# Seven stream buffers instead of five, re-used V space, four row groups for all output matmuls, and zero stores moved out of the first attention of a forward-and-backward decode kernel

## The chip, the cores and the metric

The kernel runs on one core of a Trainium2 chip. The metric is device time in microseconds (us), the median over separate executions. Before the change it was 562.25 us (555.37 to 563.79, three runs). A profiled execution records every instruction and transfer; its span (first to last instruction) is about 2 us shorter than the time of the same run.

## The reference

One token goes through two attention layers (A) and two MLP layers (B), with shared weights, and then backwards. The outputs are the final row and the gradients of the input, both caches and all weights.

```python
W = 4096                         # window: the last 4096 of 32768 cache rows
def A(x, k_cache, v_cache, wq, wo):        # 32 query heads, 4 kv heads, Dh = 128
    q = heads(x @ wq)                      # wq: 1024 x 4096
    p = softmax(q @ k[last W].T * Dh**-0.5)
    return (p @ v[last W]) @ wo            # wo: 4096 x 1024
def B(x, w1, b1, w2):                      # w1: 1024 x 3584, w2: 3584 x 1024
    h = x @ w1 + b1
    return (h * tanh(softplus(h))) @ w2
x = x + A(layernorm(x)); x = x + B(layernorm(x))      # called A1 and B2 below
x = x + A(layernorm(x)); x = x + B(layernorm(x))      # called A3 and B4
out, vjp = jax.vjp(f, A_x, k_cache, v_cache, wq, wo, w1, b1, w2)
return (out, *vjp(grad_out))               # gradients of all eight, bf16
```

Because a layer occurs twice, every weight gradient is a sum of two outer products. The cache gradients are zero outside the window: 58.7 MB of zeros (112 stores of 512 KB) must be written and depend on nothing.

## The kernel before

wq and the windows of K and V stay in SBUF, and so do NR of the sixteen 512 KB chunks of wo. All of w1, all of w2 and the other wo chunks are streamed through NB rotating buffers, anew in each pass. The loads and the zero stores are issued in program order on one queue (SP); the results leave through POOL's queue.

```python
NB = 5          # stream buffers
NR = 8          # wo chunks that stay in SBUF
strm  = tc.tile_pool(name="strm", bufs=NB)
vpool = tc.alloc_tile_pool(name="vpool", bufs=1)          # V, 32 KB per partition

def zeros(n):                          # n zero stores, from a tile that is never written again
    for _ in range(min(n, len(zero_jobs))):
        nc.sync.dma_start(zero_jobs.pop(0), zt[:])

# attention, forward, last step: y = o @ wo
order = list(range(NR, NO)) + list(range(NR))             # streamed chunks first
for i, c in enumerate(order):
    w = wo_kept[c] if c < NR else wo_load(c)
    if i == NB - 1:
        zeros(Z["A1" if first else "A3"])
    fwd_rows2(yacc, w, c, o_bf, i == 0, i == NO - 1)

# MLP, backward through w1: transpose each chunk on the matrix engine, copy it back, use it
def T(i):
    w = w1_load(i)                     # 448 KB into a stream buffer
    zeros(1 if i % 8 == 7 else 0)
    xpose2([alt_blocks(w[:, 0:1024], 4), alt_blocks(w[:, 1024:1792], 3)])   # 14 transposes
def M(i, _): ...                       # 14 matmuls of one column
pipe(list(range(2 * TD)), T, M)

Z = dict(A1=6, B2=1, A3=18, B4=1, bw2=19)
# [cut] ... after the last attention backward:
zeros(1000)                            # the final flush: all that are left

# output stage. R holds the two row vectors of a gradient at partitions 32*q, q = 0..3
def dw_tall(R, nblk, out_v):           # the gradients of w2 and wo
    for c in range(nblk // 2):
        st = stage_tile([P, 2, D], "st_t")
        pss = [psum2([P, 1024], FP32, "ops") for _ in range(2)]
        for i in range(2):
            for tt in range(2):
                b = 2 * c + tt
                outer(R, b % 4, (b // 4) * P, i * 512, pss[tt][:, i * 512:(i + 1) * 512])
        for tt in range(2):
            ev_out(st[:, tt, :], pss[tt][:])      # PSUM to SBUF on VectorE or ScalarE, in turn
        nc.gpsimd.dma_start(out_v[c], st[:])

def dkv(x3, y3, x1, y1, out_t):        # the gradients of K and V: two row groups (k = 0, 1) at a time
    for gp in range(2):
        for c0 in range(0, NC, 2):
            # [cut] two stage tiles; per four column blocks two 1024-wide PSUM tiles, 32-row matmuls at
            # row group c0 + k, two evictions of 128 x 1024; then two stores of 512 KB

stg = [0]
def stage_tile(shape, name):           # ten store tiles: five of their own, five stream buffers
    stg[0] += 1
    if stg[0] % 10 < 5:
        return shaped(pools["stage"].tile(...), shape)
    return shaped(strm.tile(...), shape)
```

Of the kernel before, what the change touches and what calls it, by code (L numbers as in the profile page):

```python
# [14 lines left out]
P = 128  # L15
HQ = 32
DH = 128
G = 4
NB = 5
NR = 8  # L20


@with_exitstack
def kernel(
# [116 lines left out]
    def shaped(t, shape):  # L141
        n = 1
        for k in shape[1:]:
            n *= k
        ap = t[0:shape[0], 0:n]
        if len(shape) == 3:
            return ap.rearrange("p (a b) -> p a b", a=shape[1])
        if len(shape) == 4:
            return ap.rearrange("p (a b c) -> p a b c", a=shape[1], b=shape[2])
        return ap  # L150

# [142 lines left out]
    def row_layout(col32, name):  # L294
        x = work.tile([P, G, DH], BF16, name=name, tag="rx", bufs=2)
        ps = psum1([P, P], BF16, "rps")
        nc.tensor.transpose(ps[:, 0:P], col32[:], ident_bf[:])
        for g in range(G):
            nc.vector.tensor_scalar(out=x[:, g, :], in0=ps[:, 0:P], scalar1=gmask[:, g:g + 1], scalar2=None, op0=ALU.mult)  # L299
        return x  # L300
# [227 lines left out]
    def attn_bwd(g_col, g_bf, lname, sv, first, nxt):  # L528
# [27 lines left out]
        big = psum2([P, WC], FP32, "big")  # L556
        rows_mm(big, pad, V_t)
        scr = work.tile([P, WC], BF16, name="scr", tag="e32", padded_shape=[P, 2 * WC])
        sdp = work.tile([P, 1], FP32, name="sdp")
# [5 lines left out]
        nc.vector.tensor_copy(sd[:], lps[:])  # L565
        ds = keep.tile([P, WC], BF16, name=f"ds_{lname}")
        nc.vector.scalar_tensor_tensor(out=ds[:], in0=big[:], scalar=sd[:, 0:1], in1=sv["p"][:], op0=ALU.subtract, op1=ALU.mult)
# [24 lines left out]
    def new_rows(name):  # L592
        return pools["rows"].tile([P, 2, 1024], BF16, name=name, tag="rows")

    def rows_put(R, side, kind, how):

        src, spread_t = pairs[kind], pools["spread"]
        spread = spread_t[:].rearrange("p j (q x) -> p j q x", q=4)
        for l in range(2):
            c = src[:, l, :]  # L600
            if how == "rep":
                nc.vector.tensor_copy(spread[:, :, :, l], c[:, :, None].to_broadcast([P, 8, 4]))
            elif how == "blocks":
                n = src.shape[2] // 4
                nc.vector.tensor_copy(spread[:, 0:n, :, l], c.rearrange("p (j q) -> p j q", q=4))
            elif how == "heads":
                for a in range(2):
                    nc.vector.tensor_copy(spread[:, 4 * a:4 * a + 4, :, l], c[:, 16 * a:16 * a + 16].rearrange("p (q b) -> p b q", q=4))
            else:
                for a in range(2):  # L610
                    v = c[:, 14 * a:14 * a + 14]
                    nc.vector.tensor_copy(spread[:, 4 * a:4 * a + 4, 0:3, l], v[:, 0:12].rearrange("p (q b) -> p b q", q=3))
                    nc.vector.tensor_copy(spread[:, 4 * a:4 * a + 2, 3, l], v[:, 12:14])
# [7 lines left out]
    def stage_tile(shape, name):  # L621
        stg[0] += 1
        if stg[0] % 10 < 5:
            return shaped(pools["stage"].tile([P, 2048], BF16, name=name, tag="so"), shape)
        return shaped(strm.tile([P, 2048], BF16, name=name, tag="st"), shape)

    def ev_out(out_ap, in_ap):
        evac(out_ap, in_ap, 1.22, 1.05)

    def outer(R, q, lo, ro, ps):  # L630
        mm(ps, R[32 * q:32 * q + 2, 0, lo:lo + P], R[32 * q:32 * q + 2, 1, ro:ro + ps.shape[1]], True, True, tile_position=(32 * q, 0))

    def dw_tall(R, nblk, out_v):

        for c in range(nblk // 2):
            st = stage_tile([P, 2, D], "st_t")
            pss = [psum2([P, 1024], FP32, "ops") for _ in range(2)]
            for i in range(2):
                for tt in range(2):
                    b = 2 * c + tt  # L640
                    outer(R, b % 4, (b // 4) * P, i * 512, pss[tt][:, i * 512:(i + 1) * 512])
            for tt in range(2):
# [3 lines left out]
    def dkv(x3, y3, x1, y1, out_t):  # L646
        ov = out_t[0, :, Sk - W:, :].rearrange("g (p t) d -> p g t d", p=P)
        for gp in range(2):
            for c0 in range(0, NC, 2):
                sts = [stage_tile([P, 2, TJ, DH], "st_kv") for _ in range(2)]  # L650
                for j4 in range(TJ // 4):
                    pss = [psum2([P, 4, 2, DH], FP32, "ops") for _ in range(2)]
                    for jj in range(4):
                        j = 4 * j4 + jj
                        for lay, (x, y) in enumerate(((x3, y3), (x1, y1))):
                            for k in range(2):
                                c = c0 + k
                                mm(pss[k][:, jj, :, :].rearrange("p g d -> p (g d)"), x[32 * c:32 * c + 32, j * P:(j + 1) * P],
                                   y[32 * c:32 * c + 32, 2 * gp:2 * gp + 2, :].rearrange("p g d -> p (g d)"), lay == 0 and jj % 2 == 0, lay == 1,
                                   tile_position=(32 * c, 0))  # L660
                    for k in range(2):
                        ev_out(sts[k][:, :, 4 * j4:4 * j4 + 4, :].rearrange("p g t d -> p t g d"), pss[k][:])
                for k in range(2):
                    nc.gpsimd.dma_start(ov[:, 2 * gp:2 * gp + 2, (c0 + k) * TJ:(c0 + k + 1) * TJ, :], sts[k][:])  # L664

    rows = {}

    def after_v():
        vpool.release()
        pools["rows"] = ctx.enter_context(tc.tile_pool(name="rows", bufs=2))  # L670
        pools["stage"] = ctx.enter_context(tc.tile_pool(name="stage", bufs=5))
        pools["spread"] = pools["rows"].tile([P, 8, P], BF16, name="spread", tag="spread", bufs=1)
        nc.gpsimd.memset(pools["spread"][:], 0.0)
        rows["w2"] = new_rows("R2")
        rows_put(rows["w2"], 0, "a", "blocks")
        rows_put(rows["w2"], 1, "gB", "rep")

    Z = dict(A1=6, B2=1, A3=18, B4=1, bw2=19)

# [66 lines left out]
    pt.release()  # L746
    pools["p2"] = ctx.enter_context(tc.tile_pool(name="p2", bufs=4, space=bass.MemoryType.PSUM))


    dw_tall(rows["w2"], TF, out_8.rearrange("(c p t) d -> c p t d", p=P, t=2))  # L750
    rows["w1"] = new_rows("R1")
    rows_put(rows["w1"], 0, "nB", "rep")
    rows_put(rows["w1"], 1, "dh", "pieces")
    for t in range(TD):
# [11 lines left out]
    rows["wo"] = new_rows("Ro")  # L766
    rows_put(rows["wo"], 0, "o", "blocks")
    rows_put(rows["wo"], 1, "gA", "rep")
    dw_tall(rows["wo"], HQ, out_5.rearrange("(c p t) d -> c p t d", p=P, t=2))
    do3 = row_layout(sA3["dorep"][:].rearrange("p c x -> p (c x)"), "do3x")  # L770
    do1 = row_layout(sA1["dorep"][:].rearrange("p c x -> p (c x)"), "do1x")
    dkv(sA3["p"], do3, sA1["p"], do1, out_3)
    q3 = row_layout(sA3["qrep"][:].rearrange("p c x -> p (c x)"), "q3x")
    q1 = row_layout(sA1["qrep"][:].rearrange("p c x -> p (c x)"), "q1x")
    dkv(sA3["ds"], q3, sA1["ds"], q1, out_2)
    rows["wq"] = new_rows("Rq")
    rows_put(rows["wq"], 0, "nA", "rep")
    rows_put(rows["wq"], 1, "dq", "heads")
    for t in range(TD):
# [39 lines left out]
```

## Time and profile before

| | before |
|---|---|
| time, median of 3 (us) | 562.25 |
| span of the profile (us) | 560.3 |
| bytes moved (MB), mean rate (GB/s) | 188.76, 337 |
| matrix engine, VectorE, ScalarE busy | 69%, 41%, 34% |
| mean granted clock of the matrix engine | 0.671 |

From the page of the kernel before: the span, busy time by engine (us, share, count), and the span in 40 equal slices: granted clock and busy share of the 16 DMA engines in tenths (9 is 90% or more), and GB/s.

```profile
span 560.3 us, 15939 instructions
PE 384.5 (69%) x7058; PEld 305.6 (55%) x7058; DVE 228.9 (41%) x411; ACT 192.4 (34%) x211; POOL 51.0 (9%) x95
...
PEclk9996555555569996677976599767755555555555
DMA  8999989999799979789599888896998978797986
GB/s 306 416 418 408 414 301 381 400 400 416 265 384 388 409 243 321 259 282 322 205 363 405 351 277 295 273 349 216 418 414 361 383 308 323 305 341 255 301 349 251
```

No engine is busy throughout. Transfers run at up to 418 GB/s, but not all the time: 188.76 MB at 415 GB/s would take 455 us, so by this estimate about 105 us of transfer time are lost, forward (slices 1 to 14) in a few gaps, backward (15 to 30) almost everywhere.

**Forward.** What the matrix engine waited for between 58 and 81 us, the last step of the first attention (columns: total, times, longest):

```profile
PE acc L188 <- DMA wo_c<-in_A_wo_dram: 16.2, 8, 8.1
```

The load queue's timeline (start, duration, what, count) shows why one wait lasts 8.1 us: six zero stores are issued between the fifth and the sixth streamed wo chunk.

```profile
47.67 5.45 SPq L255 DMA_DIRECT2D wo_c<-in_A_wo_dram  x5
54.13 6.68 SPq L129 DMA_DIRECT2D out_dram<-zt  x6
61.77 2.86 SPq L255 DMA_DIRECT2D wo_c<-in_A_wo_dram  x3
```

**Backward.** Part of the first backward w1 pass in the timeline; "tps" are the 14 transposes of a chunk, "acc" its 14 matmuls, and the brackets tell idle time before them:

```profile
244.43 0.96 PE L168 MATMUL tps<-ident_bf,w_c 128*128 128x128 bf16 x14 [1.12 <-DMA w_c<-in_B_w_dram]
245.23 0.49 PE L188 MATMUL acc<-dh_pair,w_c 128*128 128x1 bf16 x14
247.53 1.68 PE L168 MATMUL tps<-ident_bf,w_c 128*128 128x128 bf16 x14 [1.81 <-DMA w_c<-in_B_w_dram]
249.00 0.56 PE L188 MATMUL acc<-dh_pair,w_c 128*128 128x1 bf16 x14
249.42 1.65 PE L168 MATMUL tps<-ident_bf,w_c 128*128 128x128 bf16 x14
250.87 0.56 PE L188 MATMUL acc<-dh_pair,w_c 128*128 128x1 bf16 x14
```

The engine waits for loads, and after the 1.81 us wait the same 14 transposes take 1.68 instead of 0.96 us: the clock has dropped to half. At half clock the chunks' matmuls start 1.87 us apart (249.00 to 250.87); elsewhere in this pass, without waits and at full clock, 1.14 us. The windows view of both w1 passes (length, then busy time of PE, PEld, DVE, ACT, POOL with counts, granted clock, DMA share, GB/s):

```profile
235.40:263.00 27.60, 20.94 (x422) 20.34 (x420) 10.90 (x17) 10.65 (x13) 0.00 (x0) 0.81 0.84 276
346.00:373.00 27.00, 19.93 (x400) 19.24 (x397) 10.68 (x18) 10.01 (x12) 0.00 (x0) 0.81 0.88 293
```

Neither the matrix engine (20.9 of 27.6 us) nor DMA (276 GB/s) is full.

**Output.** The two groups of evictions of the w2 and wo gradients, from the groups view (count, busy us, mean ns, idle before), and one window of that stage:

```profile
L136 DVE CAST st_t<-ops 128x1024 bf16<-128x1024 f32 x28 | 33.0, 1220 | 6.9 <-issue 3.3
L139 ACT CAST st_t<-ops 128x1024 bf16<-128x1024 f32 x32 | 31.3, 1014 | 23.4 <-PE ops L188 21.6
```
```profile
430.00:440.00 10.00, 8.47 (x32) 1.56 (x32) 9.09 (x8) 9.34 (x10) 4.06 (x8) 0.50 0.81 315
```

VectorE and ScalarE are over 90% busy there, with one eviction each per chunk. In dkv the matrix engine works in two row groups; the timeline shows a pair of 256-column matmuls each 0.21 us:

```profile
496.57 0.44 PE L188 MATMUL ops<-do3x,p_A_2001 32*128 32x256 bf16 x2
496.78 0.45 PE L188 MATMUL ops<-do1x,p_A_681 32*128 32x256 bf16 x2
497.00 0.44 PE L188 MATMUL ops<-do3x,p_A_2001 32*128 32x256 bf16 x2
```

### The profile page before, as it was taken

Reading aid. Unit: us, or ns where it says so; the run is one execution under the profiler, and the core shown is the slowest. Engines: PE = TensorE matmul, PEld = TensorE weight load, DVE = VectorE, ACT = ScalarE, POOL = GpSimd, SP = SyncE. Lnnn points to the kernel's source line nnn. Section 1 sums busy time; section 2 is a strip of 40 time slices with the busy share of each in tenths; the row PEclk is TensorE's granted clock in tenths of the full one; section 3 lists DMA queues with packets and bytes.
Section 4 is the critical chain, followed back from the end, with each engine's and each line's share of the span. In section 5 each row is a group of like instructions: output and inputs, shape, how many; then the busy total and the mean of one; then the engine's idle time right before and its main releaser. Section 6 shows DMA issues by size and latency. Waiting matters only on the chain. (4 is left out here: it accounts for less than half of the span.)

```text
span 560.3 us, 15939 instructions
## 1 busy us (share of the span) xinstructions
PE 384.5 (69%) x7058; PEld 305.6 (55%) x7058; DVE 228.9 (41%) x411; ACT 192.4 (34%) x211; POOL 51.0 (9%) x95
## 2 busy tenths in 40 slices
PE   3384254364589979877966688768675756888790
PEld 3373153362589979867954677768362112146510
DVE  2052000102037753334632155324304866977691
ACT  1041000001027733333530144323102786855591
POOL 2000000000000000000000000000001423433341
PEclk9996555555569996677976599767755555555555
DMA  8999989999799979789599888896998978797986
GB/s 306 416 418 408 414 301 381 400 400 416 265 384 388 409 243 321 259 282 322 205 363 405 351 277 295 273 349 216 418 414 361 383 308 323 305 341 255 301 349 251
DMA packets 51041, 188.76 MB, mean 337 GB/s; under 512 B 5888, under 2 KB 5916, under 8 KB 49948
## 3 DMA queue, kind: packets, MB, share of 16 engines
q1 hardware_dynamic: 40624, 147.87, 69.9%
q0 software_dynamic: 10304, 39.86, 19.0%
q8 instruction: 55, 0.90, 0.6%
q14 instruction: 14, 0.11, 0.1%
q10 hardware_dynamic: 44, 0.01, 0.0%
HBM read 89.14 MB, written 98.58 MB: 335 GB/s over the span
## 5 line engine op out<-in xcount | busy, mean ns | idle before, releaser
L168 PE MATMUL tps<-ident_bf,w_c 128*128 128x128 bf16 x896 | 72.9, 246 | 16.3 <-DMA w_c<-in_B_w_dram 16.0
L188 PEld LDWEIGHTS <-w_c 128*128 128x128 bf16 x1792 | 57.8, 100 | 33.8 <-DMA w_c<-in_B_w_dram 23.8
L139 ACT COPY w_c<-tps 128x1024 bf16<-128x1024 bf16 (+1 forms) x50 | 46.2, 927 | 84.4 <-PE tps L168 79.5
L168 PEld LDWEIGHTS <-w_c 128*128 128x128 bf16 x896 | 62.8, 112 | 17.9 <-DMA w_c<-in_B_w_dram 17.9
L136 DVE COPY w_c<-tps 128x1024 bf16<-128x1024 bf16 (+1 forms) x70 | 46.0, 667 | 64.6 <-PE tps L168 60.8
L139 ACT CAST st_t<-ops 128x1024 bf16<-128x1024 f32 x32 | 31.3, 1014 | 23.4 <-PE ops L188 21.6
L136 DVE CAST st_t<-ops 128x1024 bf16<-128x1024 f32 x28 | 33.0, 1220 | 6.9 <-issue 3.3
L188 PEld LDWEIGHTS <-wo_c 128*128 128x128 bf16 x512 | 16.4, 102 | 22.6 <-DMA wo_c<-in_A_wo_dram 21.8
L188 PE MATMUL acc<-a_pair,w_c 128*128 128x1 bf16 x448 | 15.8, 165 | 17.2 <-DMA w_c<-in_B_w_dram 12.3
L209 ACT ACTIVATE lnv<-var,eps_t 128x1 f32<-128x1 f32 x4 | 1.2, 294 | 72.5 <-DVE var L206 72.5
L168 PE MATMUL tps<-ident_bf,wo_c 128*128 128x128 bf16 x256 | 21.2, 249 | 5.6 <-DMA wo_c<-in_A_wo_dram 5.6
L188 PE MATMUL acc<-nB_pair,w_c 128*128 128x1 bf16 x448 | 15.8, 165 | 12.4 <-DMA w_c<-in_B_w_dram 9.3
L589 POOL DMA_DIRECT2D out_dram<-rt x2 | 1.2, 594 | 251.3 <-DVE rt L588 224.4
L188 PE MATMUL acc<-o_pair,wo_c 128*128 128x1 bf16 x256 | 8.7, 166 | 21.2 <-DMA wo_c<-in_A_wo_dram 20.9
L136 DVE COPY wo_c<-tps 128x1024 bf16<-128x1024 bf16 x20 | 13.7, 691 | 21.2 <-PE tps L168 20.6
L136 DVE CAST st_kv<-ops 128x1024 bf16<-128x1024 f32 x15 | 18.3, 1225 | 9.8 <-PE ops L188 7.0
L139 ACT CAST st_kv<-ops 128x1024 bf16<-128x1024 f32 x17 | 17.0, 1014 | 14.4 <-PE ops L188 14.4
L168 PEld LDWEIGHTS <-wo_c 128*128 128x128 bf16 x256 | 18.3, 113 | 6.0 <-DMA wo_c<-in_A_wo_dram 6.0
L139 ACT COPY wo_c<-tps 128x1024 bf16<-128x1024 bf16 x12 | 12.1, 1012 | 22.3 <-PE tps L168 21.1
L188 PE MATMUL ops<-Ro 2*128 2x512 bf16 x64 | 16.8, 602 | 3.1 <-ACT st_t L139 1.9
L644 POOL DMA_DIRECT2D out_dram<-st_t x30 | 16.0, 534 | 26.5 <-DVE st_t L136 18.1
L136 DVE CAST st_wq<-ops 128x1024 bf16<-128x1024 f32 x15 | 17.2, 1217 | 1.8 <-ACT st_wq L139 0.8
(501 smaller groups left out, 708.2 us busy)
## 6 DMA issues: line engine op xcount, KB each, us to landing
out_dram<-zt SPq DMA_DIRECT2D x112, 512.0 KB, 8.7
w_c<-in_B_w_dram SPq DMA_DIRECT2D x64, 448.0 KB, 5.6
w_c<-in_B_w_dram SPq DMA_DIRECT2D x42, 512.0 KB, 5.9
wo_c<-in_A_wo_dram SPq DMA_DIRECT2D x32, 512.0 KB, 7.6
out_dram<-st_t POOLq DMA_DIRECT2D x30, 512.0 KB, 4.9
out_dram<-st_kv POOLq DMA_DIRECT2D x16, 512.0 KB, 5.2
out_dram<-st_wq POOLq DMA_DIRECT2D x16, 512.0 KB, 5.1
K_180<-in_A_k_cache_dram SPq DMA_DIRECT2D x1, 1024.0 KB
```

The costliest lines, as they stand in the source:

```text
L136: nc.vector.tensor_copy(out_ap, in_ap)
L139: nc.scalar.copy(out_ap, in_ap)
L168: nc.tensor.transpose(ps[:, b, :], ap, ident_bf[:])
L188: nc.tensor.matmul(out_ap, lhsT=lhsT, rhs=rhs, start=start, stop=stop, skip_group_check=True, **kw)
L209: nc.scalar.activation(lnv[:], var[:], ACT.Ln, bias=eps_t[:, 0:1], scale=1.0)
L589: nc.gpsimd.dma_start(out_flat.rearrange("(n p) -> n p", p=P), rt[0:n, :])
L644: nc.gpsimd.dma_start(out_v[c], st[:])
```

## The change

The intent: more loads in flight (seven stream buffers). Space for them comes from one kept wo chunk and from V's region, which is free once the last attention backward has used V; the last ds tile, the row tiles and the staging pool move there. The rest rearranges the output matmuls over four row groups and moves zero stores.

```diff
-NB = 5
-NR = 8
+NB = 7
+NR = 7
 ...
+        if not first:                            # V has just been read for the last time
+            vpool.release()
+            pools["late"] = ctx.enter_context(tc.tile_pool(name="late", bufs=1))
-        ds = keep.tile([P, WC], BF16, name=f"ds_{lname}")
+        ds = (keep if first else pools["late"]).tile([P, WC], BF16, name=f"ds_{lname}")
 ...
-        return pools["rows"].tile([P, 2, 1024], BF16, name=name, tag="rows")
+        return pools["rows"].tile([P, 3, 1024], BF16, name=name, tag="rows", bufs=2)
 ... (rows_put: for w2 and wo three parts instead of two are built, transposed and copied)
-        if stg[0] % 10 < 5:
+        if stg[0] % 10 in (0, 3, 6):             # three staging buffers and seven stream buffers
 ...
-                    b = 2 * c + tt
-                    outer(R, b % 4, (b // 4) * P, i * 512, pss[tt][:, i * 512:(i + 1) * 512])
+                    outer(R, 2 * i + tt, c * P, i * 512, pss[tt][:, i * 512:(i + 1) * 512])
 ... (dkv, new: four 512 KB stage tiles at once)
+            for j2 in range(TJ // 2):
+                pss = [one 512-wide PSUM tile for each c of NC]          # pool of 8
+                for jj, layer, c: mm(pss[c][:, jj], x[32*c:32*c+32, j*P:(j+1)*P], y[32*c:...], tile_position=(32*c, 0))
+                for c in range(NC):
+                    evac(sts[c][...], pss[c], 0.69, 0.6)
+            for c in range(NC):
+                nc.gpsimd.dma_start(ov[...], sts[c][:])
 ... (the row tiles q3 and q1 are now built ahead of both dkv calls, not between them)
-    Z = dict(A1=6, B2=1, A3=18, B4=1, bw2=19)
+    Z = dict(A1=0, B2=1, A3=14, B4=1, bw2=18)
```

With the changed number of streamed chunks this leaves 41 zero stores for the final flush instead of 31.

More of the change, by code (lines that the diff above doesn't have):

```diff
@@ L149, in shaped @@
             return ap.rearrange("p (a b c) -> p a b c", a=shape[1], b=shape[2])
+        if len(shape) == 5:
+            return ap.rearrange("p (a b c d) -> p a b c d", a=shape[1], b=shape[2], c=shape[3])
         return ap
@@ L294, in row_layout @@
     def row_layout(col32, name):
-        x = work.tile([P, G, DH], BF16, name=name, tag="rx", bufs=2)
+        x = pools["late"].tile([P, G, DH], BF16, name=name, tag="rx", bufs=4)
         ps = psum1([P, P], BF16, "rps")
@@ L592, in new_rows, with rows_put @@
     def new_rows(name):
-        return pools["rows"].tile([P, 2, 1024], BF16, name=name, tag="rows")
-    def rows_put(R, side, kind, how):
+        return pools["rows"].tile([P, 3, 1024], BF16, name=name, tag="rows", bufs=2)
+    def rows_put(R, side, kind, how, part=0):
         src, spread_t = pairs[kind], pools["spread"]
@@ L603, in rows_put @@
             elif how == "blocks":
-                n = src.shape[2] // 4
-                nc.vector.tensor_copy(spread[:, 0:n, :, l], c.rearrange("p (j q) -> p j q", q=4))
+                v = c.rearrange("p (j q) -> p j q", q=2)[:, 8 * part:min(8 * part + 8, src.shape[2] // 2), :]
+                for k in range(2):
+                    nc.vector.tensor_copy(spread[:, 0:v.shape[1], 2 * k:2 * k + 2, l], v)
             elif how == "heads":
@@ L630, in outer @@
     def outer(R, q, lo, ro, ps):
-        mm(ps, R[32 * q:32 * q + 2, 0, lo:lo + P], R[32 * q:32 * q + 2, 1, ro:ro + ps.shape[1]], True, True, tile_position=(32 * q, 0))
+        L = R[:, 1:, :].rearrange("p a b -> p (a b)")
+        mm(ps, L[32 * q:32 * q + 2, lo:lo + P], R[32 * q:32 * q + 2, 0, ro:ro + ps.shape[1]], True, True, tile_position=(32 * q, 0))
     def dw_tall(R, nblk, out_v):
@@ L648, in dkv @@
         for gp in range(2):
-            for c0 in range(0, NC, 2):
-                sts = [stage_tile([P, 2, TJ, DH], "st_kv") for _ in range(2)]
-                for j4 in range(TJ // 4):
-                    pss = [psum2([P, 4, 2, DH], FP32, "ops") for _ in range(2)]
-                    for jj in range(4):
-                        j = 4 * j4 + jj
-                        for lay, (x, y) in enumerate(((x3, y3), (x1, y1))):
-                            for k in range(2):
-                                c = c0 + k
-                                mm(pss[k][:, jj, :, :].rearrange("p g d -> p (g d)"), x[32 * c:32 * c + 32, j * P:(j + 1) * P],
-                                   y[32 * c:32 * c + 32, 2 * gp:2 * gp + 2, :].rearrange("p g d -> p (g d)"), lay == 0 and jj % 2 == 0, lay == 1,
-                                   tile_position=(32 * c, 0))
-                    for k in range(2):
-                        ev_out(sts[k][:, :, 4 * j4:4 * j4 + 4, :].rearrange("p g t d -> p t g d"), pss[k][:])
-                for k in range(2):
-                    nc.gpsimd.dma_start(ov[:, 2 * gp:2 * gp + 2, (c0 + k) * TJ:(c0 + k + 1) * TJ, :], sts[k][:])
+            sts = [stage_tile([P, 2, TJ, DH], "st_kv") for _ in range(NC)]
@@ new lines, in dkv @@
+            for j2 in range(TJ // 2):
+                pss = []
+                for c in range(NC):
+                    pss.append(shaped(pools["p1"].tile([P, 512], FP32, name="ops", tag="p1"), [P, 2, 2, DH]))
+                for jj in range(2):
+                    j = 2 * j2 + jj
+                    for lay, (x, y) in enumerate(((x3, y3), (x1, y1))):
+                        for c in range(NC):
+                            mm(pss[c][:, jj, :, :].rearrange("p g d -> p (g d)"), x[32 * c:32 * c + 32, j * P:(j + 1) * P],
+                               y[32 * c:32 * c + 32, 2 * gp:2 * gp + 2, :].rearrange("p g d -> p (g d)"), lay == 0 and jj == 0, lay == 1,
+                               tile_position=(32 * c, 0))
+                for c in range(NC):
+                    evac(sts[c][:, :, 2 * j2:2 * j2 + 2, :].rearrange("p g t d -> p t g d"), pss[c], 0.69, 0.6)
@@ L666 @@
+            for c in range(NC):
+                nc.gpsimd.dma_start(ov[:, 2 * gp:2 * gp + 2, c * TJ:(c + 1) * TJ, :], sts[c][:])
     rows = {}
     def after_v():
-        vpool.release()
-        pools["rows"] = ctx.enter_context(tc.tile_pool(name="rows", bufs=2))
-        pools["stage"] = ctx.enter_context(tc.tile_pool(name="stage", bufs=5))
-        pools["spread"] = pools["rows"].tile([P, 8, P], BF16, name="spread", tag="spread", bufs=1)
+        pools["rows"] = ctx.enter_context(tc.tile_pool(name="rows", bufs=1))
@@ L673, in after_v @@
+        pools["stage"] = ctx.enter_context(tc.tile_pool(name="stage", bufs=3))
+        pools["spread"] = pools["rows"].tile([P, 8, P], BF16, name="spread")
         nc.gpsimd.memset(pools["spread"][:], 0.0)
         rows["w2"] = new_rows("R2")
-        rows_put(rows["w2"], 0, "a", "blocks")
-        rows_put(rows["w2"], 1, "gB", "rep")
-    Z = dict(A1=6, B2=1, A3=18, B4=1, bw2=19)
+        rows_put(rows["w2"], 0, "gB", "rep")
+        for part in range(2):
+            rows_put(rows["w2"], 1 + part, "a", "blocks", part)
@@ L746 @@
     pt.release()
-    pools["p2"] = ctx.enter_context(tc.tile_pool(name="p2", bufs=4, space=bass.MemoryType.PSUM))
+    pools["p2"] = tc.alloc_tile_pool(name="p2", bufs=4, space=bass.MemoryType.PSUM)
     dw_tall(rows["w2"], TF, out_8.rearrange("(c p t) d -> c p t d", p=P, t=2))
     rows["w1"] = new_rows("R1")
-    rows_put(rows["w1"], 0, "nB", "rep")
-    rows_put(rows["w1"], 1, "dh", "pieces")
+    rows_put(rows["w1"], 1, "nB", "rep")
+    rows_put(rows["w1"], 0, "dh", "pieces")
     for t in range(TD):
@@ L766 @@
     rows["wo"] = new_rows("Ro")
-    rows_put(rows["wo"], 0, "o", "blocks")
-    rows_put(rows["wo"], 1, "gA", "rep")
+    rows_put(rows["wo"], 0, "gA", "rep")
+    for part in range(2):
+        rows_put(rows["wo"], 1 + part, "o", "blocks", part)
     dw_tall(rows["wo"], HQ, out_5.rearrange("(c p t) d -> c p t d", p=P, t=2))
@@ L771 @@
     do1 = row_layout(sA1["dorep"][:].rearrange("p c x -> p (c x)"), "do1x")
-    dkv(sA3["p"], do3, sA1["p"], do1, out_3)
     q3 = row_layout(sA3["qrep"][:].rearrange("p c x -> p (c x)"), "q3x")
     q1 = row_layout(sA1["qrep"][:].rearrange("p c x -> p (c x)"), "q1x")
+    pools["p2"].release()
+    pools["p1"] = tc.alloc_tile_pool(name="p1", bufs=8, space=bass.MemoryType.PSUM)
+    dkv(sA3["p"], do3, sA1["p"], do1, out_3)
     dkv(sA3["ds"], q3, sA1["ds"], q1, out_2)
+    pools["p1"].release()
+    pools["p2"] = ctx.enter_context(tc.tile_pool(name="p2b", bufs=4, space=bass.MemoryType.PSUM))
     rows["wq"] = new_rows("Rq")
-    rows_put(rows["wq"], 0, "nA", "rep")
-    rows_put(rows["wq"], 1, "dq", "heads")
+    rows_put(rows["wq"], 1, "nA", "rep")
+    rows_put(rows["wq"], 0, "dq", "heads")
     for t in range(TD):
```

## The prediction

> **What bounds the kernel now.** The windows view gives three regimes.
> (1) Forward, 0 to 200 us: transfers. DMA runs at 370 to 420 GB/s; I take 415 as full speed, 1.26 us per 512 KB chunk. In the first attention the matrix engine waits 16.2 us for wo chunks, one wait 8.1 us long (waits view, 58 to 81 us): the queue's timeline shows six zero stores issued between the fifth and the sixth streamed wo chunk.
> (2) Backward, 200 to 429 us: buffer turnaround. In both w1 passes (233 to 267, 344 to 375 us) a 448 KB chunk takes 1.93 us, although DMA could bring it in 1.1 us and the matrix engine, at full clock, works it off in 1.14 us (timeline). A load lands 5.6 us after issue; with about 4 us of use, five buffers give 9.6/5 = 1.9 us. The waits also let the granted clock drop to half, where a chunk takes 1.86 us. The Trainium skill (TensorE: Matmul & The Clock Gate, Part 1) says idling of about 3.4 us throttles the clock; the trace agrees in kind (clock 0.50 to 1.00 in these stages).
> (3) Output, 429 to 560 us: evictions and stores near balance. A two-block chunk takes 1.24 us; its evictions take 1.22 us on VectorE and 1.01 on ScalarE. Exceptions: dkv (16 chunks in 30.6 us, 1.9 us each), where two row groups finish a matmul pair every 0.213 us, so 256 matmuls need 27 us; row-tile setups of 4 to 5 us, where DMA drains; and about 10 us of final drain.
>
> **What the change does.**
> - A1 without zeros: the last wo chunks no longer queue behind 6 x 1.26 us. Nine are streamed, seven prefetched. About 8 us, plus 2 to 3 us of the gap at 80 to 90 us (278 GB/s). A3 has four zeros fewer, but its compute chain hides most: 1 to 3 us. Forward gain about 12 us.
> - Seven buffers: turnaround 9.6/7 = 1.37 us. Each w1 pass loses 8 to 10 us; the w2 passes and wo streams 2 to 3 us each. Backward gain about 27 us.
> - One wo chunk less kept: 4 x 0.5 MB more reads, 5 us of DMA, mostly in slack. Ten zeros (12.6 us of DMA) move to the final flush, 31 to 41 stores; they overlap the first output stage, filling its setup gap, and ten staging buffers absorb the rest.
> - Four row groups in the dw stages: nearly nothing. The Trainium skill (TensorEngine Tiling, PSUM Bottleneck) says tiling speeds the matmuls, not PSUM eviction; the trace shows VectorE and ScalarE over 90% busy there.
> - dkv: quads every 0.213 us need 14 us; 64 half-width evictions at about 0.69 and 0.6 us (an estimate between measured widths) then limit at 20 to 24 us. Gain 7 to 10 us.
> - Lost: three row-tile builds instead of two for w2 and wo, 2 us each.
>
> **Sum.** Output stage starts near 391 us instead of 429, takes about 126 instead of 131: about 518 us.
>
> **Predicted: 518 us, range 502 to 540.** Faster by over 2%: 0.95; within 2%: 0.04; slower: 0.01.
>
> **What would show it.** First nB matmul near 70 us (80.9 before); w1 passes at 1.2 to 1.4 us per chunk with clock above 0.85; first st_t eviction near 391 us (429.9); dkv under 25 us; eviction busy time in dw stages unchanged; zero stores overlapping st_t stores.
>
> **What would make it wrong.** Landing time growing with seven loads outstanding, so DMA bounds the w1 passes; the clock staying low; zeros at the end slowing the first output stage by their whole 12 us; PSUM banks or eviction overhead eating dkv's gain.

## The result and the profile after

The changed kernel takes 516.0 us (514.95 to 518.7, four runs); the kernel before took 563.02 us (four runs). The ratio is 0.9241, 95% interval 0.9126 to 0.9357. All outputs are right. Executions over 1.5% slower than the fastest of the same kernel are left out of the means. A ratio is the mean time of one kernel's fast runs over that of the other's of the same rounds, so it is not quite the ratio of the medians quoted: here two of the four runs of the kernel before (563.79 and 563.88 us) were slow, and the mean of the other two is 558.8 us.

```profile
span 513.4 us, 16036 instructions
PE 364.3 (71%) x7090; PEld 287.1 (56%) x7090; DVE 229.6 (45%) x440; ACT 194.8 (38%) x230; POOL 51.3 (10%) x95
...
PEclk9997555556559989898985599876555555555555
DMA  8999999999599979899999799999999999979996
GB/s 290 414 420 412 407 372 405 408 410 416 191 382 415 412 315 358 303 377 406 385 415 415 264 343 375 400 354 416 416 414 404 400 392 354 360 297 317 376 381 236
```

These are the same lines of the page of the changed kernel. It moves 190.33 MB. At 415 GB/s that is 459 us, so the lost transfer time falls from an estimated 105 to 55 us, while 1.6 MB more are moved. The matrix engine's busy time falls by 20 us though it has 32 more matmuls: more of its work runs at full clock.

The span can be cut into stages without remainder, at the moments when VectorE first writes each layer's normalised or gradient column. In us, one profile each; "control" is a second profile of the changed kernel, and the two columns on the right anticipate experiments:

| stage | before | changed | control | five buffers | six buffers |
|---|---|---|---|---|---|
| A1 (loads, attention, wo) | 80.4 | 72.7 | 72.7 | 72.7 | 72.7 |
| B2 | 39.2 | 36.0 | 36.7 | 39.2 | 37.4 |
| A3 | 41.0 | 38.4 | 38.6 | 41.9 | 40.4 |
| B4, with its backward w2 | 72.2 | 69.3 | 69.7 | 72.5 | 69.7 |
| w1 pass of B4, backward | 32.5 | 21.7 | 24.1 | 30.7 | 25.8 |
| A3 backward | 54.5 | 51.2 | 50.1 | 56.7 | 54.8 |
| w2 pass of B2, backward | 24.0 | 20.1 | 21.2 | 22.5 | 21.7 |
| w1 pass of B2, backward | 30.9 | 22.5 | 23.5 | 31.3 | 27.9 |
| A1 backward | 52.3 | 51.5 | 51.3 | 54.2 | 51.4 |
| to the first output eviction | 2.9 | 2.5 | 2.5 | 2.5 | 2.5 |
| output stage | 130.4 | 127.5 | 127.2 | 127.2 | 126.2 |
| sum | 560.3 | 513.4 | 517.6 | 551.4 | 530.5 |

The forward part (first three rows) gained 13.5 us, the rest up to the output stage 30.5 us (26.9 in the control) and the output stage 2.9 us. A caution for reading such differences: four profiles of kernels that are identical up to the output stage (changed, control, and two experiments below) begin it at 385.9, 390.4, 382.5 and 385.2 us. From there to the end the profiles repeat better (127.5 and 127.2 us for changed and control, 127.2 with five buffers).

Forward, the load queue now issues all nine wo chunks without zeros between them. The waits for wo chunks between 58 and 73 us shrank from 16.2 to 5.5 us; here first the wait, then the queue's timeline:

```profile
PE acc L190 <- DMA wo_c<-in_A_wo_dram: 5.5, 8, 0.7
```
```profile
46.47 12.50 SPq L257 DMA_DIRECT2D wo_c<-in_A_wo_dram  x9
59.91 7.97 SPq L268 DMA_DIRECT2D w_c<-in_B_w_dram  x7
67.94 0.42 SPq L129 DMA_DIRECT2D out_dram<-zt  x1
```

Backward, the w1 pass is now a regular beat of 1.14 us per chunk with one short wait in the stretch shown, and both passes run at full clock with transfers at 381 GB/s (timeline, then windows):

```profile
222.61 0.94 PE L170 MATMUL tps<-ident_bf,w_c 128*128 128x128 bf16 x14
223.39 0.49 PE L190 MATMUL acc<-dh_pair,w_c 128*128 128x1 bf16 x14
223.75 0.94 PE L170 MATMUL tps<-ident_bf,w_c 128*128 128x128 bf16 x14
224.53 0.49 PE L190 MATMUL acc<-dh_pair,w_c 128*128 128x1 bf16 x14
225.62 0.96 PE L170 MATMUL tps<-ident_bf,w_c 128*128 128x128 bf16 x14 [0.61 <-DMA w_c<-in_B_w_dram]
```
```profile
217.70:236.00 18.30, 17.17 (x418) 16.83 (x419) 10.90 (x17) 10.89 (x13) 0.00 (x0) 1.00 1.00 381
311.00:330.00 19.00, 17.26 (x417) 16.73 (x414) 10.79 (x18) 10.64 (x13) 0.00 (x0) 1.00 1.01 381
```

In the output stage, the mean eviction is as long as before (1218 and 1020 ns). DMA is full in the first stretch, and there is something new: the tile view of the store tiles st_t says that evictions and stores waited 13.1 us for earlier stores to free their buffers; in the kernel before that view has no such line.

```profile
L139 ACT CAST st_t<-ops 128x1024 bf16<-128x1024 f32 x33 | 32.2, 1020 | 23.8 <-PE ops L190 15.3
L136 DVE CAST st_t<-ops 128x1024 bf16<-128x1024 f32 x27 | 31.4, 1218 | 7.5 <-PE ops L190 3.0
```
```profile
386.00:406.00 20.00, 12.82 (x56) 2.75 (x52) 15.40 (x15) 14.50 (x15) 6.45 (x12) 0.50 1.02 403
```
```profile
  DMA out_dram<-st_t: 13.1, 8
```

In dkv, four row groups finish four matmuls in the 0.21 us that two took before, as long as PSUM tiles are free:

```profile
456.60 0.42 PE L190 MATMUL ops<-do3x,p_A_1995 32*128 32x256 bf16 x4
456.82 0.42 PE L190 MATMUL ops<-do1x,p_A_679 32*128 32x256 bf16 x4
457.03 0.42 PE L190 MATMUL ops<-do3x,p_A_1995 32*128 32x256 bf16 x4
```

The st_kv evictions now start over a stretch of 21.3 us (457 to 478); before it was 27.1 us.

### The profile page after: what moved, and what is told of

The parts are those of the page before. It is cut to its first block, busy times and chain, and to the rows that moved or that the text cites. A ratio compares the mean times of both kernels' runs of the same rounds, so it can differ in the third digit from the quotient of the medians.

```text
span 513.4 us, 16036 instructions
## 1 busy us (share of the span) xinstructions
PE 364.3 (71%) x7090; PEld 287.1 (56%) x7090; DVE 229.6 (45%) x440; ACT 194.8 (38%) x230; POOL 51.3 (10%) x95
## 2 busy tenths in 40 slices
DMA packets 51473, 190.33 MB, mean 371 GB/s; under 512 B 5936, under 2 KB 5964, under 8 KB 50380
## 4 chain that ended last, share of the span: by engine, by line
PE 48%; DMA 28%; DVE 9%; ACT 6%; issue 5%; SPq 1%; POOL 0%; POOLq 0%; ACTq 0%; DVEq 0%
PE tps L170 19%; PE acc L190 16%; DMA w_c<-in_B_w_dram 9%; PE ops L190 7%; DMA wo_c<-in_A_wo_dram 5%; DMA wo_196<-in_A_wo_dram 4%; DMA K_180<-in_A_k_cache_dram 2%; DMA out_dram<-st_t 2%; PE big L190 2%; DMA wq_0_164<-in_A_wq_dram 2%; DMA out_dram<-st_kv 1%; DVE st_t L136 1%; PE rw L623 1%; DMA out_dram<-st_w_8287 1%; DVE st_kv L136 1%
## 5 line engine op out<-in xcount | busy, mean ns | idle before, releaser
L190 PEld LDWEIGHTS <-w_c 128*128 128x128 bf16 x1792 | 56.3, 99 | 29.7 <-DMA w_c<-in_B_w_dram 19.4
L170 PE MATMUL tps<-ident_bf,w_c 128*128 128x128 bf16 x896 | 63.9, 228 | 2.2 <-DMA w_c<-in_B_w_dram 2.2
L170 PEld LDWEIGHTS <-w_c 128*128 128x128 bf16 x896 | 55.0, 103 | 2.7 <-DMA w_c<-in_B_w_dram 2.7
L139 ACT CAST st_t<-ops 128x1024 bf16<-128x1024 f32 x33 | 32.2, 1020 | 23.8 <-PE ops L190 15.3
L136 DVE CAST st_t<-ops 128x1024 bf16<-128x1024 f32 x27 | 31.4, 1218 | 7.5 <-PE ops L190 3.0
L190 PEld LDWEIGHTS <-wo_c 128*128 128x128 bf16 x576 | 18.1, 101 | 15.1 <-DMA wo_c<-in_A_wo_dram 12.5
L190 PE MATMUL acc<-a_pair,w_c 128*128 128x1 bf16 x448 | 15.8, 165 | 13.5 <-DMA w_c<-in_B_w_dram 8.6
L136 DVE COPY wo_c<-tps 128x1024 bf16<-128x1024 bf16 x22 | 14.9, 690 | 14.5 <-PE tps L170 12.1
L139 ACT COPY wo_c<-tps 128x1024 bf16<-128x1024 bf16 x14 | 14.2, 1012 | 18.5 <-PE tps L170 16.2
L139 ACT CAST st_kv<-ops 128x512 bf16<-128x512 f32 x34 | 17.9, 592 | 8.5 <-PE ops L190 6.2
L136 DVE CAST st_kv<-ops 128x512 bf16<-128x512 f32 x30 | 18.4, 683 | 4.0 <-PE ops L190 2.4
L139 ACT CAST st_wq<-ops 128x1024 bf16<-128x1024 f32 x18 | 17.5, 1022 | 5.9 <-PE ops L190 5.0
L623 PE MATMUL rw<-ident_bf,spread 128*128 128x128 bf16 x80 | 10.3, 310 | 12.7 <-DVE spread L607 6.4
L170 PEld LDWEIGHTS <-wo_c 128*128 128x128 bf16 x288 | 18.4, 105 | 0.0
```

The source lines that it names most:

```text
L136: nc.vector.tensor_copy(out_ap, in_ap)
L139: nc.scalar.copy(out_ap, in_ap)
L170: nc.tensor.transpose(ps[:, b, :], ap, ident_bf[:])
L190: nc.tensor.matmul(out_ap, lhsT=lhsT, rhs=rhs, start=start, stop=stop, skip_group_check=True, **kw)
L623: nc.tensor.transpose(ps[:, j, :], spread_t[:, j, :], ident_bf[:])
```

## The experiments

Each experiment is an edit of the changed kernel, if not said otherwise. The theory on trial is the prediction's sum of separate terms: buffer turnaround (about 30 us), zeros out of the way (about 9), dkv (7 to 10), row groups in dw_tall (nothing), losses of about 4. The rivals attribute the gain otherwise or deny a term. Times of the kernel before in the same calls had medians of 559.5, 558.9 and 560.3 us, so the medians of different calls compare within some 2 us.

| run | median us (range) | ratio to before | 95% interval |
|---|---|---|---|
| control_after | 517.09 (515.53 to 519.48) | 0.9231 | 0.9166 to 0.9296 |
| two_groups_dw | 516.61 (512.59 to 522.33) | 0.9208 | 0.9134 to 0.9281 |
| a1_zeros_back | 517.52 (516.59 to 518.81) | 0.9250 | 0.9196 to 0.9304 |
| dkv_old | 518.93 (515.98 to 519.81) | 0.9264 | 0.9206 to 0.9323 |
| five_buffers | 551.80 (549.35 to 556.11) | 0.9902 | 0.9830 to 0.9975 |
| six_buffers | 532.46 (530.37 to 535.96) | 0.9554 | 0.9492 to 0.9616 |
| before_new_zeros | 558.00 (556.19 to 559.73) | 1.0005 | 0.9948 to 1.0062 |
| zeros_in_gaps | 512.82 (510.76 to 514.48) | 0.9193 | 0.9137 to 0.9250 |
| eight_buffers | 510.86 (508.68 to 514.04) | 0.9112 | 0.9059 to 0.9166 |
| six_kept | 519.86 (513.73 to 520.57) | 0.9250 | 0.9194 to 0.9305 |
| rows_early | 521.83 (516.94 to 524.50) | 0.9296 | 0.9239 to 0.9353 |
| rows_early_zeros_in_gaps | 518.52 (516.93 to 522.93) | 0.9262 | 0.9207 to 0.9317 |

### The control

No edit.

> The changed kernel once more, as the control for this chip. Both theories: 515 to 519 us, ratio to the kernel before 0.915 to 0.93.

Measured 517.09 us, ratio 0.9231, as expected.

### Two row groups again in dw_tall

```diff
-                    outer(R, 2 * i + tt, c * P, i * 512, pss[tt][:, i * 512:(i + 1) * 512])
+                    outer(R, 2 * (c % 2) + tt, c * P, i * 512, pss[tt][:, i * 512:(i + 1) * 512])
```

> Changed kernel, but the four matmuls of a dw_tall chunk (w2 and wo gradients) use two row groups, as before the change. My theory: eviction and stores limit these stages, so 0 to +2 us on the control (516 to 520), the busy time of VectorE and ScalarE on st_t unchanged (about 31 and 32 us). Rival: the matmuls were on the chain in these two stages (30 chunks), so +4 to +8 us, with longer waits of the evictions for the matmuls.

Measured 516.61 us, 0.5 us below the control (its 522.33 us is a slow run): the rival is out. The evictions keep their medians of 1012 and 1223 ns; the output stage of the profile takes 128.2 us (control 127.2), within the 0 to 2 us of my theory. Four row groups in these two stages are worth nothing measurable.

### Six zero stores back in the first attention

```diff
-    Z = dict(A1=0, B2=1, A3=14, B4=1, bw2=18)
+    Z = dict(A1=6, B2=1, A3=14, B4=1, bw2=18)
```

> Changed kernel with the six zero stores back in the first attention (35 instead of 41 left for the final flush). My theory: the first w1 matmul comes 7 to 9 us later (73.2 us in the changed kernel), but the final flush is 7.6 us of transfers shorter, so the first output stage loses most of its waits for staging buffers (12.6 us in one stretch); net +3 to +6 us. Rival 1: transfers bound the whole kernel, so moving six stores changes nothing (-1 to +1). Rival 2: the flush at the end is free, so the whole 7 to 9 us stay.

Measured 517.52 us, 0.4 us on the control: rival 1, against my theory and the prediction. The trace shows both sides of the trade. The first w1 matmul starts at 80.4 us instead of 73.2, so the forward gain is real; the output stage is 3.7 us shorter than the control's (123.5 us), and the waits for st_t buffers are all but gone (control 14.0 us), as the same line of the tile view says:

```profile
  DMA out_dram<-st_t: 0.6, 1
```

The remaining 3 us or so lie within the spread of the stages between. A store that need not be made early still has to be made, and here the place to which it was moved was full.

### The old dkv

```diff
-    pools["p2"].release()
-    pools["p1"] = tc.alloc_tile_pool(name="p1", bufs=8, space=bass.MemoryType.PSUM)
     dkv(...)        # and the body of dkv as in the kernel before
```

> Changed kernel with the old dkv (two row groups, 1024-wide tiles in four PSUM buffers, stores by twos). My theory: from the first to the last st_kv eviction 27 to 29 us instead of 21.8, so +5 to +8 us on the control. Rival: dkv is limited by the staging buffers and the stores (the changed kernel waits for st_kv stores and DMA drops to 232 GB/s there), so +0 to +3 us.

Measured 518.93 us, +1.8 us; the intervals of the two ratios overlap. From the first to the last start of an st_kv eviction it takes 24.4 us instead of 20.8 (control), so the new dkv saves some 3.6 us inside the stage. The saving is still there at the end of the profile: the output stage takes 131.6 us against 127.2 (control) and 127.5 (changed). That the median shows only 1.8 us fits the spread of the part before, which is the same in these kernels and began the output stage at 385.2 us here and at 390.4 in the control. So the new dkv is worth some 2 to 4 us, less than my theory's 5 to 8 and about the upper end of the rival's 0 to 3. The rest of what the stage gained against the kernel before (27.1 us) came without it: the old dkv takes 24.4 us when the q tiles are built ahead of it, though this build then lengthens the gap before dkv by 0.5 us (4.1 to 4.6 us from the last start of an st_t eviction to the first of st_kv).

### Five and six stream buffers

```diff
-NB = 7
+NB = 5
-        if stg[0] % 10 in (0, 3, 6):
+        if stg[0] % 10 < 5:
-        pools["stage"] = ctx.enter_context(tc.tile_pool(name="stage", bufs=3))
+        pools["stage"] = ctx.enter_context(tc.tile_pool(name="stage", bufs=5))
```

(for six: NB = 6, four staging buffers, the pattern (0, 3, 6, 8); ten store tiles in all, always)

> Changed kernel with five stream buffers instead of seven (five staging buffers instead of three, so ten in all as before). My theory, buffer turnaround: the w1 passes go back to 1.8 to 2.0 us per chunk, the output stage starts 15 to 25 us later than in the control (385 to 390 us), total 530 to 542 us. Rival: the gain came from the zeros' places and from the output stage, and five buffers would do: +0 to +8 us, 516 to 525.

> Changed kernel with six stream buffers and four staging buffers. Turnaround 9.6/6 gives 1.6 us per chunk of the w1 passes where buffers limit, so between: 522 to 530 us. A rival that the gain is a threshold (the matrix engine either keeps its full clock or not): equal to seven buffers or equal to five.

Five buffers take 551.8 us, 34.7 more than the control; six take 532.46, 15.4 more. Both lie above the ranges that I expected (530 to 542 and 522 to 530 us). The rival of the first run is out by far: with five buffers and everything else of the change, only 7 of 42 us are left (5.5 by the ratio, whose interval is 1.4 to 9.5). The gain is the buffers, more than my theory's 15 to 25 us, and it comes by steps of 19.3 and 15.4 us, no threshold. One thing goes along with it: NB also says after which load the zero stores of Z are issued (`if i == NB - 1`), so with fewer buffers they stand one or two loads earlier. What that does was not tested apart. The stage table shows where: 14.4 us in the two w1 passes (62.0 against 47.6 in the control), and one to seven more in each of the other stages that stream after the first: B2 2.5, A3 3.3, B4 2.8, A3 backward 6.6, the w2 pass 1.3, A1 backward 2.9. The output stage does not change.

The first w1 pass, from the start of the first chunk's matmuls to that of the last chunk's, divided by 15 steps: 1.78 us per chunk in the kernel before, 1.75 with five buffers, 1.37 with six, 1.18 with seven (control 1.29). In the second pass it is 1.76, 1.80, 1.53 and 1.23 (control 1.30). The windows of both passes with five buffers and, for the first pass, with six:

```profile
227.60:255.00 27.40, 22.25 (x421) 21.55 (x420) 10.95 (x18) 10.90 (x13) 0.00 (x0) 0.75 0.92 304
338.00:366.00 28.00, 20.20 (x409) 19.46 (x406) 10.90 (x19) 10.43 (x13) 0.00 (x0) 0.88 0.89 293
```
```profile
222.50:244.00 21.50, 18.00 (x423) 17.39 (x420) 11.00 (x18) 10.65 (x13) 0.00 (x0) 0.98 0.95 332
```

Clock and waits fall and rise together, though not in step: 0.75 and 0.88 with five buffers, 0.98 and 0.89 with six, 1.00 and 1.00 with seven (0.97 and 0.91 in the control). Which share of the gain is waiting and which is the lower clock that the waiting brings was not separated by an experiment, but the traces give an estimate. From five buffers to the control, the waits for w_c in the two passes fall from 11.7 to 3.1 us, 8.6 us less, and the time at half clock, from the granted clock of the passes, falls from about 19.4 to 4.5 us. At half clock a chunk takes 1.87 instead of 1.14 us, so each us at half clock loses some 0.39 us, 5.8 us in all. The sum, 14.4 us, is what the stage table shows: about three fifths are waits and two fifths the clock. In the first pass of the kernel before it is 6.2 us of waits, and four chunks that run at half clock, some 3 us.

### The kernel before, with the zeros moved only

```diff
 (in the kernel before)
-    Z = dict(A1=6, B2=1, A3=18, B4=1, bw2=19)
+    Z = dict(A1=0, B2=1, A3=14, B4=1, bw2=18)
```

> Kernel before, with only the zero stores moved as in the change (none in the first attention, 14 and 18 later, 10 more in the final flush). After the run with the six zeros put back, I expect moved stores to be conserved: forward 7 to 9 us earlier, final flush 12.6 us longer, total within 6 us of the kernel before (ratio 0.99 to 1.01). Rival (my prediction's sum): the forward gain stays, -8 to -10 us, ratio 0.982 to 0.986.

Measured 558.0 us, ratio 1.0005: conserved within the interval of about 3 us either way. In the profile the output stage starts 7.6 us earlier (422.3 us against 429.9) and is 3.6 us longer (134.0 us). Of these 7.6 us, 7.2 are in A1 (73.2 us); B2 and A3 take 39.4 and 40.5 us, about as before. This and a1_zeros_back say the same in both kernels: the zeros' new place is no gain that these runs can see.

### Zero stores in the idle stretches

```diff
-    Z = dict(A1=0, B2=1, A3=14, B4=1, bw2=18)
+    Z = dict(A1=0, B2=1, A3=18, B4=1, bw2=21)
```

> Changed kernel with four more zero stores in the second attention (DMA at 142 GB/s from 130 to 140 us) and three more before the backward w2 pass (182 GB/s from 290 to 300 us), so 34 in the final flush instead of 41. If idle transfer time is what counts, these seven stores are free where they go and the flush is 8.8 us shorter: -4 to -8 us on the control (509 to 513), with no waits for st_t buffers in the first output stage. Rival: they delay the loads behind them by as much as they save, -1 to +2.

Measured 512.82 us, 4.3 below the control's median. But the ratios are 0.9193 and 0.9231 with intervals that overlap widely, so 2 to 4 us are likely and nothing is certain. The stretch from the first to the last st_t eviction is 62.0 us instead of 65.6 and the whole output stage 123.6 instead of 127.2, with no waits for st_t stores left, as it should be with a shorter flush.

### Eight stream buffers, six kept wo chunks

```diff
-NB = 7
-NR = 7
+NB = 8
+NR = 6
```

(three staging buffers as in the changed kernel, so eleven store tiles)

> Changed kernel with eight stream buffers and six kept wo chunks (what space allows). Five to six to seven buffers gave -19 and -15 us. My theory: with seven the w1 passes already run at 1.14 to 1.2 us per chunk, the matrix engine's own pace, so the eighth buffer has little left to give (the waits for w_c and wo_c in the backward part add up to under 5 us) and costs 2.1 MB of reads (5 us of transfers): -3 to +3 us on the control (514 to 520). Rival, the trend: -8 to -14 us (503 to 509).

Measured 510.86 us, ratio 0.9112, about 6 us below the control: neither theory. My reason held in part, my sum did not. The w1 passes have little left to gain: 1.21 us per chunk in both, with 0.3 us of waits for w_c in all and two gaps of 1.5 and 1.0 us for which the profile shows no cause, against 1.18 and 1.23 in the changed kernel (1.29 and 1.30 in the control). The windows:

```profile
218.00:236.00 18.00, 16.30 (x404) 16.13 (x401) 10.70 (x17) 10.29 (x13) 0.00 (x0) 1.00 0.98 359
311.00:330.00 19.00, 17.45 (x424) 16.90 (x420) 10.94 (x18) 11.08 (x14) 0.00 (x0) 1.00 0.98 359
```

The gain lies before the output stage, which begins at 382.3 us (control 390.4, changed 385.9); its largest part is A1 backward (47.6 us instead of 51.3). The output stage as a whole is not shorter (127.4 us, control 127.2): the stretch from its first eviction to its last is (111.5 us instead of 114.8), but then the stores drain for 15.9 us instead of 12.4. So these profiles show no gain from the eleventh store tile. Of all versions run this has the lowest median, below both kernels, though its interval overlaps that of zeros_in_gaps. A closer comparison than the control is the next run.

### Six kept wo chunks alone

```diff
-NR = 7
+NR = 6
```

> Changed kernel with six kept wo chunks instead of seven, seven buffers: the price of one kept chunk alone, 2.1 MB more reads, 5.0 us of transfers at full rate, and one more transposed chunk in the last attention. My theory: mostly on the chain now, since DMA is idle for only about 55 us in all: +2 to +6 us (519 to 523). Rival (the prediction's words, mostly in slack): 0 to +2 us.

Measured 519.86 us, ratio 0.9250 against the control's 0.9231: +1 to +3 us, with overlapping intervals. Unclear; a chunk less kept costs a few us at most. It moves 191.90 MB, 1.57 MB more than the changed kernel: three more reads of 512 KB, not four, because a kept chunk has to be read once too. (The prediction and the expectations of this run and the last counted four.)

This run is eight_buffers with one stream buffer, and so one store tile, less: 519.86 against 510.86 us, ratios 0.9250 and 0.9112 with intervals that do not overlap. The eighth buffer with its store tile is thus worth some 8 to 9 us, not 6. The output stages are alike (126.9 and 127.4 us); in these two profiles the gain is 3.5 us in the w1 passes, 1.8 in A3 backward, 2.3 in A1 backward and most of the rest in B2 and A3. So the steps are 19, 15 and 8 to 9 us: they shrink, but do not end where the w1 passes reach the matrix engine's pace.

### Row tiles built earlier

Between the last eviction of one output stage and the first of the next, the row tiles of the next stage are built: spread on VectorE, transposed on the matrix engine, copied out. This edit moves each build into the stage before.

```diff
+    rows["w1"] = new_rows("R1"); rows_put(...)          # moved ahead of dw_tall for w2
     dw_tall(rows["w2"], ...)
-    rows["w1"] = new_rows("R1"); rows_put(...)
     for t in range(TD):
         for hf in range(2):
+            if t == 4 and hf == 0:
+                put_o()                                  # Ro, in the middle of w1's stage
 ...
-    dw_tall(rows["wo"], HQ, out_5...)
+    dw_tall(rows["wo"], HQ, out_5..., {5: put_q, 10: put_x})   # Rq, then the do and q tiles
```

> Changed kernel with every row-tile build of the output stage taken out of the gap between two stages and put into the middle of the stage before (w1's before w2's stage, wo's inside w1's, wq's and the do and q tiles inside wo's). The gaps between the last eviction of one stage and the first of the next are 5.4 us twice and about 4 us twice. If these gaps are on the chain: -6 to -12 us on the control (505 to 511). Rival: stores bound the output stage and drain during the gaps, so -3 to +1.

Measured 521.83 us, 4.7 slower than the control, with ratios whose intervals overlap, and far from the 6 to 12 us that I expected to gain. The gaps between the stages did shrink (2.3 us before dkv, 1.4 before wq), but the evictions now stop in the middle of a stage. The timeline, while put_o runs:

```profile
423.93 1.03 PE L623 MATMUL rw<-ident_bf,spread 128*128 128x128 bf16 x8 [1.64 <-DVE spread L607]
425.00 0.69 DVE L136 COPY Ro<-rw 128x1024 bf16<-128x1024 bf16 x1 [1.13 <-PE rw L623]
...
428.25 1.03 PE L623 MATMUL rw<-ident_bf,spread 128*128 128x128 bf16 x8 [1.12 <-DVE spread L612]
429.32 1.01 ACT L139 COPY Ro<-rw 128x1024 bf16<-128x1024 bf16 x1 [5.91 <-PE rw L623]
429.93 8.64 DVE L136 CAST st_w<-ops 128x1024 bf16<-128x1024 f32 x8 [1.74 <-issue]
```

ScalarE idles 5.91 us, as long as in a gap. The evictions stand behind the build in the program, and the trace shows them going on only after its last copy has begun (429.32 and 429.93 us): the serial chain over three engines stops them where it stands. From the first to the last eviction the output stage takes 115.5 us against 114.8 in the control; its stores then drain for 17.1 us instead of 12.4. And w1's build, now ahead of the first eviction, delays that: 5.1 us after the last gradient column instead of 2.5. My theory falls in this form; an interleaving of single steps of the build with evictions remains untried.

### Both, and more zeros in gaps

```diff
+ (the edit of rows_early)
-    Z = dict(A1=0, B2=1, A3=14, B4=1, bw2=18)
+    Z = dict(A1=0, B2=1, A3=18, B4=1, bw2=21)
-                    zeros(c % 2)         # forward w2 pass of B4
+                    zeros(1)
```

> The same with the zero stores of the gap run, and six more in the second w2 pass of the forward part (DMA at 319 GB/s there), so 28 in the final flush. With fewer evictions held up and a flush 16 us shorter: 498 to 506 us. Rival: output stage bound by stores, 508 to 514.

Measured 518.52 us: not the predicted 498 to 506, and outside the rival's range too. It is 3.3 us below rows_early, the order of size that zeros_in_gaps showed; thirteen fewer stores in the flush do not bring their 16 us of transfer time.

## Why the prediction was right, and where its sum was not

The time was predicted as 518 us and measured as 516.0. Point by point:

- **What bounds the kernel: right.** Buffer turnaround bounded the backward part; five_buffers and six_buffers show it.
- **"Backward gain about 27 us": right.** Measured 30.5 us (26.9 in the control); each w1 pass lost 8.4 to 10.8 us (7.4 and 8.4 in the control), where "8 to 10" stood. The turnaround formula was somewhat too simple: 9.6/7 = 1.37 us was predicted per chunk and 1.18 to 1.30 measured, 9.6/6 = 1.6 and 1.37 and 1.53 measured. It leaves out that the first chunks of a pass are already there when it begins: the first wait for w_c in the first pass stands before the sixth chunk with five buffers, the eighth with six, the ninth with seven. A load does land later with more of them outstanding (median 5.6 us before, 6.6 after, for 448 KB). With seven buffers the DMA engines are busy throughout these passes (share 1.00), but only 0.9 and 1.4 us of waits for w_c are left, so this has little left to bound.
- **"Forward gain about 12 us": right as a stage time** (13.5 us), **wrong as a net gain.** Of it 7.7 us come from the six zero stores, and putting them back costs 0.4 us of the time. The step that failed is that the moved stores "overlap the first output stage, filling its setup gap, and ten staging buffers absorb the rest". The buffers did not absorb them: evictions and stores waited 13.1 us for st_t stores. The prediction's own list of what could go wrong has the point ("zeros at the end slowing the first output stage"). The other 5.8 us of the forward gain are the buffers' (the columns for five buffers and control: 5.8 us in B2 and A3), where the prediction put 3 to 6 us of them down to the zeros (the gap at 80 to 90 us and A3); with the zeros alone moved, B2 and A3 gained 0.3 us.
- **dkv: mechanism right, size too large.** "Gain 7 to 10 us": the stage is 5.8 us shorter (27.1 to 21.3), within the 20 to 24 us named as its limit, but undoing the rewrite alone costs 3.6 us in the stage, 4.4 in the output stage and 1.8 in the median time.
- **Four row groups in the dw stages, "nearly nothing": right** (-0.5 us when undone). The Trainium skill (TensorEngine Tiling (Array Packing), section PSUM Bottleneck) says that tiling speeds up the matmuls but not the copies out of PSUM; this agrees, with evictions of 1.22 and 1.01 us that do not change.
- **The clock: right.** 0.81 became 1.00 in both w1 passes (0.97 and 0.91 in the control; "above 0.85" was the test). The Trainium skill (TensorE: Matmul & The Clock Gate, Part 1) has two states, half and full, and a drop after an idle window of about 3.4 us. The trace agrees with the two states (14 transposes in 1.68 or 0.94 us), but in the w1 pass of the kernel before the drops came after scattered waits of 0.9 to 1.8 us, not after one long one.

So the sum came out right partly because errors cancelled: the buffers are worth 34.7 us by the experiment, where the prediction had about 30, and the zeros are worth nothing, where it had about 9. Effects of undoing single parts need not add up; of the 42 us some 6 are assigned to no part, or 3 if dkv is counted with its 4.4 us of the output stage.

## What to carry to other kernels

Where both the engine and DMA are part idle and each chunk waits for its load, divide the time that a buffer is held (issue to landing plus use) by the number of buffers: if that exceeds the slower of transfer and work, another buffer is worth the space, and the matrix engine's clock recovers with the waits. Take the quotient as a rough figure: it was 5 to 17% above the measured time per chunk here, and the eighth buffer still gained in the kernel's other stages after these passes had all but reached the engine's pace. Work that nothing depends on, moved off a chain, is a gain only if the place where it ends up has room: look at the transfers and the store buffers there first. A serial chain over several engines was not hidden by moving it earlier in the program; it stopped the evictions there.

## What the Trainium skill lacked or had wrong

- DMA: Bandwidth & Descriptors has no word on how the landing time grows with the number of outstanding loads of one queue. Here the median from issue to landing of a 448 KB load was 5.3 us with five buffers, 6.2 with six, 6.6, 6.9 and 7.2 in three kernels with seven (changed, control, six_kept) and 7.2 with eight.
- TensorE: Matmul & The Clock Gate, Part 1 and the section on HAM oscillation, tell of idle gaps above about 3 us; the page's one passage on short idles (the second failure mode) gives no length for them. Here a pass with five waits for loads of at most 1.8 us (6.2 us in 27) fell to half clock for some chunks.
- TensorE: Matmul & The Clock Gate, Part 4, says that transposes do not engage the full clock. In the w1 passes of the changed kernel half of the matmuls are transposes (against an identity), with two thirds of the time, and the granted clock is 1.00 throughout: 14 transposes take 0.94 us, against 1.68 at half clock. Whether transposes alone would keep the clock up, no run here shows.
- TensorEngine Tiling (Array Packing) gives only theoretical factors for row groups, 2 and 4, and no measured step from two groups to four. In dkv, two groups finish two and four groups finish four 256-column matmuls in the same 0.21 us, at half clock.
